# Mixture of experts behind a gated attention: experts 2 to 7 dealt out by their counts, the last three with 768 slots instead of 832

## The chip, the core and the metric

The kernel is one program on one core of a Trainium2 chip. The metric is the device time of one execution in microseconds (us), the median of the runs shown.

## The reference

A recurrent, gated attention (4 sequences, 8 heads, 768 steps, head size 40) gives 3072 rows `x` of 320 numbers. Each row is then sent to two of eight experts:

```
logits = x @ w_gate
noisy_logits = logits + np.log1p(np.exp(x @ w_noise)) * noise
top2 = np.argpartition(-noisy_logits, 2, axis=1)[:, :2]
top2_w = softmax of the two chosen noisy logits
for e in range(8):
    for k in range(2):
        mask = top2[:, k] == e
        h = np.maximum(x[mask] @ w1[e], 0.0)          # 320 -> 1024
        out[mask] += top2_w[mask, k, None] * (h @ w2[e])   # 1024 -> 320
```

There are 6144 choices, 768 for an expert on average. How many an expert gets (its count) is known only once the rows have been routed.

## The kernel before, in words

The attention runs in 24 units of 128 rows. While it runs, VectorE routes the rows (`g_part`): it finds the two best experts of each row and the row's rank within its expert, and a few one-hot matmuls turn expert and rank into a table TBL, 128 partitions by 8 x 7 columns: slot s of expert e stands in column 7e + s // 128, partition s % 128, and holds the row's number, or 0 where the slot is vacant. `decode` (L447) makes of columns of TBL the row numbers TOK, the choice masks KM and two helpers; vacant slots get a number beyond the last row.

An expert has a fixed number of slots, NT = 832 = 448 + 384, whatever its count: six tiles of 128 rows and one of 64 (`tiles`, L726; `rows_of`, L732). Its work:

- `gather` (L704): GpSimd's indirect DMAs fetch the rows of each tile (a vacant slot fetches nothing) into XG.
- `turn_x` and `spread_x` (L895, L902): VectorE transposes 32 x 32 blocks into XB, and 16 DMAs on SP's queue carry them to XT; `split_x` (L909) splits XT into a high part XH (ScalarE) and a low part XL (VectorE).
- `mm1` (L921): for each of the two halves of the slots (`parts`, L681) and each of eight blocks of 128 hidden units, eight matmuls (products of high and low parts) as wide as the half, 448 or 384 columns, at L931. ScalarE takes the high part HH of the result (L940), VectorE the low part HLO (L943). Of the 448 columns 64 go to HT instead (L950, L951), for the 64-row tile.
- `mm2` (L953): a tile of 128 rows is 24 matmuls of 320 columns (L960 to L962); the 64-row tile is 16, on HT (L968, L969), with ScalarE and VectorE adding its two halves (L970, L971). L973 applies the gate, `put` (L979) adds the 128 rows to the output by an indirect DMA.

Everything is written by hand into each engine's instruction stream, in the order of the text. While expert e is in `mm1` and `mm2`, the other engines prepare e + 1: its weights W1 go by SP's queue into RAW1 and are split at L149 and L150 (`split_w1`); W2 goes into RAW2 (`load_w2`, L686, issued after the first tile of e's `mm2`) and is split at L722 and L723 at the start of e + 1. The rows of e + 1 are gathered at the start of e, turned one tile after each `mm1` block from block 6 on (TURN), and split two steps at a time behind the third and later tiles of e's `mm2`. In `mm2` the tiles go in the order OR1 = 0, 6, 1, 2, 3, 4, 5.

Experts 0 and 1 are special: they begin while the routing still runs. Expert 0 is worked through in three parts (slots to 384, to 640, to 832) as the routing of rows advances; `advance` (L998) calls `decode` for a part when the table is done so far, the last call taking all columns from slot 640 of expert 0 to the end of expert 7. Expert 1 has halves of 512 and 320.

If an expert's count is over 832, a value `flag` (L614, read at L1129) sends the program through a slow loop over all experts (L1162) for the rows left over.

Of the kernel before, what the change touches and what calls it, by code (L numbers as in the profile page):

```python
# [7 lines left out]
F32 = mybir.dt.float32  # L8
# [50 lines left out]
def build(ctx, tc, qk, vk, fi, noise, wgn, w1, w2, cst, ce, out):  # L59
# [74 lines left out]

    def load_w1(e, ks=((0, 2), 2)):
        for k in ks:
            if k == 2:
                for p in range(2):
                    SP.dma_start(RAW1[64 * p:64 * p + 64, 2], w1[e, 256:320])
            else:  # L140
                a, b = k
                SP.dma_start(RAW1[:, a:b], w1[e, a * 128:b * 128].rearrange("(k p) f -> p k f", p=128))

    def split_w1(lo):
        for f in range(0, FF, 512):
# [45 lines left out]
    def run(steps):  # L191
        for _ in steps:
            pass
# [243 lines left out]
    def bc_part(t, b, late=False):  # L437
        if b:
# [5 lines left out]
                P.tensor_add(TBL, TBL, s)  # L444
            done[0] += len(b[0]) // 2

    def decode(a, b, more=True):  # L447

        t, n = TBL[:, a:b], slice(a, b)
        V.scalar_tensor_tensor(VC[:, n], t, 0.0, cs[:, C_VAC + a:C_VAC + b], op0=OP.is_equal, op1=OP.mult)  # L450
        V.scalar_tensor_tensor(AB[:, n], t, -1.0, t, op0=OP.mult, op1=OP.max)
        V.tensor_scalar(KM[:, n, 0], t, 0.0, None, op0=OP.is_gt)
        x = AB[:, n]
        if more:
            far = rt.tile([128, b - a], F32, name=f"far{a}", bufs=1)
            V.tensor_scalar(far, x, 0.5, FIT // 2, op0=OP.mult, op1=OP.add)
            x = rt.tile([128, b - a], F32, name=f"near{a}", bufs=1)
            V.scalar_tensor_tensor(x, AB[:, n], 0.0, far, op0=OP.add, op1=OP.min)
        V.scalar_tensor_tensor(TOK[:, n], x, -1.0, VC[:, n], op0=OP.add, op1=OP.add)
        V.tensor_scalar(KM[:, n, 1], t, 0.0, None, op0=OP.is_lt)  # L460

    def lc_part(i, t, w):
        u = i - 2
# [21 lines left out]
    def g_part(g):  # L485
# [121 lines left out]
        if u0 + nb == NU:  # L607
            V.tensor_add(rk[:, 0:1], rk[:, 0:1], bump[0])
            yield
            V.scalar_tensor_tensor(rk[:, 0:8], cs[:, C_I8:C_I8 + 8], -4096.0, rk[:, 0:8], op0=OP.mult, op1=OP.add)  # L610
            yield
            V.tensor_reduce(dd[:, 0:1], rk[:, 0:8], AX.X, OP.max)
            yield
            V.tensor_copy(flag, dd[:, 0:1])  # L614
# [64 lines left out]
        return psum.tile([128, 512], F32, name=name, bufs=2 if name in ("s0", "s1") else 1)  # L679

    def parts(e):  # L681
        s = (E0S, (0, 512, NT))[e] if e < 2 else (0, CA, NT)
        return [slice(a, b) for a, b in zip(s, s[1:])]


    def load_w2(e):  # L686
        SP.dma_start(RAW2, w2[e].rearrange("(j p) c -> p j c", p=128))

    def token(e, t):
        return TOK[0:rows_of(t), TC * e + t:TC * e + t + 1]  # L690
# [211 lines left out]
    def spread_x():  # L902
# [6 lines left out]
    def split_x():  # L909
        for h in range(2):  # L910
            c = slice(QO[2 * h], QO[2 * h] + 2 * QC[2 * h])
            fx = lambda a: a[:, c].rearrange("p (q t c) -> p q t c", q=2, c=32)
            fh = lambda a: a[:, c].rearrange("p (t q c) -> p q t c", q=2, c=32)
            for k in range(3):
                n = slice(0 if k < 2 else 64, 128)
                A.activation(fh(XH[n, k]), fx(XT[n, k]), AF.Copy)
                o = XL[:, k] if k < 2 else XH[0:64, 2]
                V.tensor_sub(fh(o), fx(XT[n, k]), fh(XH[n, k]).bitcast(F32))
                yield
# [137 lines left out]
    for f in range(8):  # L1057
        mm1(0, 1, f)
        advance(0.5, 2)
    assert done[0] == NU  # L1060
    load_w2(1)
    gather(1, ts=tiles(0, 1))
    for t in held:
# [22 lines left out]
    for e in range(1, NE):  # L1086
# [4 lines left out]
        for h in range(2):  # L1091
            for f in range(8):
# [22 lines left out]
        xs = split_x()  # L1115
        for n, t in enumerate(OR1):
            put(e, t, mm2(e, t))
            if e + 1 < NE:
                if not n:
# [40 lines left out]
                             in_=y[0:n], in_offset=None, compute_op=OP.add)  # L1160

    with tc.If(most > NT):  # L1162
        V.memset(ec, 0.0)
        with tc.For_i(0, NE, 1) as e:
            weights(e)
            x = xf[0:CS, 0:RW]
            tok = m2.tile([128, 1], I32, name="ftk")
            km = m2.tile([128, 2], F32, name="fkm")
            SP.dma_start(tok[0:CS], TOK[CS:128].rearrange("p (e c) -> p e c", e=NE)[:, bass.ds(e, 1), TC - 1:TC].rearrange("p e c -> p (e c)"))
            SP.dma_start(km[0:CS], KM[CS:128].rearrange("p (e c) k -> p e c k", e=NE)[:, bass.ds(e, 1), TC - 1].rearrange("p e k -> p (e k)"))  # L1170
            P.indirect_dma_start(out=x, out_offset=None, in_=XD, in_offset=bass.IndirectOffsetOnAxis(ap=tok[0:CS], axis=0),
                                 bounds_check=NTOK - 1, oob_is_err=False)
            V.tensor_mul(km[0:CS], km[0:CS], x[:, DM:DM + 2])
            V.tensor_add(km[0:CS, 0:1], km[0:CS, 0:1], km[0:CS, 1:2])
            plain(x, CS, km[0:CS, 0:1], tok[0:CS])
            V.tensor_scalar(ec, ec, 1.0, None, op0=OP.add)

        with tc.If(most > BLK):
            V.memset(ec, 0.0)
# [98 lines left out]
```

## Time and profile before

| | us |
|---|---|
| median of 3 runs | 543.9 (542.6 to 544.37) |
| span of the profiled execution, first to last instruction | 545.7 |
| TensorE busy in it | 521.9 |
| VectorE busy | 361.6 |
| ScalarE busy | 255.1 |
| GpSimd busy | 227.9 |

The profiled execution has no time of its own beside its span; the span is 1.8 us over the median of the runs. In the profile PE is TensorE's matmuls, PEld its weight loads, DVE VectorE, ACT ScalarE, POOL GpSimd and SP the engine that issues most DMAs; L931 is line 931 of the kernel. A row of a timeline gives start, duration, engine, line, operation and shapes, and in brackets how long the engine had been idle before it and what ended the wait. A matmul's duration overlaps that of the next; what it costs is the distance from one start to the next.

### The profile page before, as it was taken

To read this page: it belongs to the slowest core of one execution; us is meant where nothing else is said; L and a number is where in the kernel's file an instruction comes from. 1 tells how busy PE (TensorE), PEld (TensorE's weight loads), DVE (VectorE), ACT (ScalarE), POOL (GpSimd) and SP (SyncE) were. 2 spreads that over 40 slices of the span, in tenths; PEclk is the share of its full clock that TensorE was granted. 3 is DMA by queue.
4 is the path that set the end of the run, shared out by engine and by line. 5 is a ranking of instruction groups with operands and counts; after the bars stand their busy time and mean duration, and the time that the engine had idled before them with its cause. 6 is when DMAs were issued, how large, how long until landed. Compare 5 with 4: busy or idle time off the path is not lost.

```text
span 545.7 us, 13298 instructions
## 1 busy us (share of the span) xinstructions
PE 521.9 (96%) x5100; PEld 486.9 (89%) x5101; DVE 361.6 (66%) x983; ACT 255.1 (47%) x634; POOL 227.9 (42%) x282
## 2 busy tenths in 40 slices
PE   8889998988999899999999999999999999999995
PEld 3778887877989798999999999999999999999994
DVE  8988999998786377764854675485467548546411
ACT  8858877877614154432541543254154325415300
POOL 7445463164112837056224705632570563251043
PEclk9979999998999999999999999999999999999998
DMA  5898787897767626088159418614941771461033
GB/s 147 216 229 221 205 227 189 199 223 197 264 191 236 106 41 194 10 170 225 39 97 261 93 35 231 136 47 81 270 97 31 194 171 49 92 144 21 1 36 47
DMA packets 49797, 77.25 MB, mean 142 GB/s; under 512 B 10281, under 2 KB 39664, under 8 KB 49728
## 3 DMA queue, kind: packets, MB, share of 16 engines
q1 hardware_dynamic: 38464, 57.39, 37.9%
q0 software_dynamic: 11264, 18.95, 19.0%
q8 instruction: 42, 0.69, 0.5%
q14 instruction: 27, 0.22, 0.1%
HBM read 52.49 MB, written 17.73 MB: 129 GB/s over the span
## 4 chain that ended last, share of the span: by engine, by line
PE 73%; DVE 20%; issue 2%; DMA 1%; ACT 1%; POOL 1%; POOLq 0%; DVEq 0%; SPq 0%; ACTq 0%
PE s L931 24%; PE e L931 12%; PE o L960 5%; PE o L961 5%; PE o L962 5%; PE st L961 5%; PE st L960 4%; PE st L962 4%; DVE p L348 3%; DVE ob L602 2%; DVE kd L342 2%; DVE tm L382 1%; PE o L371 1%; PE st L969 1%; PE st L968 1%
## 5 line engine op out<-in xcount | busy, mean ns | idle before, releaser
L983 POOL DMA_INDIRECT y_out<-y,tok x56 | 92.3, 1647 | 194.8 <-DVE y L973 191.2
L940 ACT ACTIVATE hh<-s 128x384 fp32r<-128x384 f32 (+3 forms) x91 | 42.7, 470 | 83.0 <-PE s L931 80.7
L931 PE MATMUL s<-xh,w1h 128*128 128x384 f32 (+5 forms) x273 | 78.6, 345 | 0.9 <-DVE xh L743 0.8
L709 POOL DMA_INDIRECT xg<-rows,tok x56 | 63.0, 1125 | 29.2 <-issue 15.1
L931 PE MATMUL s<-xh,w1l 128*128 128x384 f32 (+5 forms) x273 | 64.3, 343 | 0.6 <-DVE xh L743 0.6
L943 DVE SCALAR_TENSOR_TENSOR hlo<-s,hh 128x384 fp32r<-128x384 f32 (+3 forms) x91 | 47.5, 522 | 20.1 <-ACT hh L940 16.6
L961 PE MATMUL o<-w2l,hh 128*128 128x320 f32 x192 | 59.8, 311 | 0.0
L960 PE MATMUL o<-w2h,hh 128*128 128x320 f32 x192 | 59.7, 311 | 0.0
L962 PE MATMUL o<-w2h,hlo 128*128 128x320 f32 x192 | 59.1, 308 | 0.0
L931 PEld LDWEIGHTS s<-xh,w1h 128*128 128x128 f32 x273 | 49.2, 188 | 4.0 <-ACT hh L940 1.0
L961 PE MATMUL st<-w2l,hh 128*128 128x320 f32 x168 | 52.3, 311 | 0.3 <-issue 0.3
L960 PE MATMUL st<-w2h,hh 128*128 128x320 f32 x168 | 52.1, 310 | 0.0
L962 PE MATMUL st<-w2h,hlo 128*128 128x320 f32 x168 | 51.7, 308 | 0.0
L931 PEld LDWEIGHTS s<-xh,w1l 128*128 128x128 f32 x273 | 48.4, 188 | 3.2 <-DVE xh L743 0.9
L931 PE MATMUL s<-xl,w1h 128*128 128x384 f32 (+5 forms) x182 | 47.6, 343 | 0.0
L383 POOL TENSOR_TENSOR xr<-tm,vk 128x320 f32<-128x320 f32 x24 | 21.3, 887 | 52.9 <-DVE tm L382 10.6
L973 DVE TENSOR_SCALAR y<-o,gw 128x320 f32<-128x320 f32 x24 | 13.2, 550 | 42.3 <-PE o L962 42.3
L931 PE MATMUL e<-xh,w1h 128*128 128x384 f32 (+5 forms) x135 | 39.6, 348 | 0.4 <-DVE ht L951 0.3
L973 DVE TENSOR_SCALAR y<-st,gw 128x320 f32<-128x320 f32 x21 | 11.6, 551 | 41.2 <-PE st L962 41.1
L940 ACT ACTIVATE hh<-e 128x384 fp32r<-128x384 f32 (+3 forms) x45 | 21.3, 473 | 34.6 <-PE e L931 24.9
L960 PEld LDWEIGHTS o<-w2h,hh 128*128 128x128 f32 x192 | 36.1, 188 | 0.3 <-DVE y L973 0.2
L962 PEld LDWEIGHTS o<-w2h,hlo 128*128 128x128 f32 x192 | 36.2, 188 | 0.0
(222 smaller groups left out, 1303.3 us busy)
## 6 DMA issues: line engine op xcount, KB each, us to landing
vk<-vk_in SPq DMA_DIRECT2D x48, 242.0 KB
raw<-w_in SPq DMA_DIRECT2D x7, 1280.0 KB
qk<-qk_in SPq DMA_DIRECT2D x48, 160.0 KB
raw<-w_in SPq DMA_DIRECT2D x7, 1024.0 KB
raw<-w_in SPq DMA_DIRECT2D x19, 256.0 KB
y_out<-zrow SPq DMA_DIRECT2D x15, 320.0 KB
xt__2782<-xb SPq DMA_DIRECT2D x24, 84.0 KB
rows<-xr POOLq DMA_DIRECT2D x12, 160.0 KB
```

The source lines that it names most:

```text
L342: V.tensor_mul(KD[u], VKS[u % 4][:, :, 328:648].rearrange("p x (h d) -> p x h d", h=H), W[u][:, :, :, L - 1:L].to_broadcast([128, 2, H, D]))
L348: V.tensor_mul(PP[u], SQ[u], W[u])
L383: P.tensor_mul(XR[u], tm.rearrange("p h d -> p (h d)"), SG[u % 4])
L709: P.indirect_dma_start(out=XG[0:rows_of(t), t], out_offset=None, in_=XD[0:n], in_offset=bass.IndirectOffsetOnAxis(ap=token(e, t), axis=0), ...
L931: T.matmul(ps[:, 0:n], l, r, start=i == 0, stop=i == len(ops) - 1)
L940: A.activation(hi, x, AF.Relu)
L943: V.scalar_tensor_tensor(lo, x, 0.0, hi.bitcast(F32), op0=OP.max, op1=OP.subtract)
L960: T.matmul(ps, HH[:, j, c], W2H[:, j], start=j == 0, stop=False)
L961: T.matmul(ps, HH[:, j, c], W2L[:, j], start=False, stop=False)
L962: T.matmul(ps, HLO[:, j, c], W2H[:, j], start=False, stop=j == 7)
L973: V.tensor_scalar(y[0:n], ps[0:n], GW[e][0:n, t:t + 1], None, op0=OP.mult)
L983: st = P.indirect_dma_start(out=out, out_offset=bass.IndirectOffsetOnAxis(ap=token(e, t), axis=0), in_=y[0:n], in_offset=None, compute_op= ...
```

## The change

On chip, as soon as the counts are known, VectorE ranks experts 2 to 7 by count (`POS`; ties go by number). `WHO` holds the expert at each rank, `SEL` is the permutation as a 6 x 6 one-hot. The places 2 to 7 of the program, which were experts 2 to 7, now stand for the experts by falling count: `deal` permutes the columns of TBL into TBP, and these are decoded. Weights are addressed by a register that SP loads from WHO. Places 2, 3 and 4 (`is_long`) keep 832 slots in 448 + 384; places 5, 6 and 7 have 768 slots in 384 + 384, six tiles, no 64-row tile. `flag` is taken from the counts with 64 added for the three short places, so that the slow loop is entered when a count is over 832 or that of a short place over 768. (That loop also changes: it takes up to 128 rows of each expert. It is left out of the diff.)

The decoding of places 2 to 7 moves: it was in the last `decode`, during the second part of expert 0, and now stands one step after each block of expert 0's third part.

```diff
     def load_w1(e, ks=((0, 2), 2)):
         for k in ks:
+            w = w1[weights_of(e)]
             if k == 2:
                 for p in range(2):
-                    SP.dma_start(RAW1[64 * p:64 * p + 64, 2], w1[e, 256:320])
+                    SP.dma_start(RAW1[64 * p:64 * p + 64, 2], w[:, 256:320].rearrange("e p f -> p (e f)"))
...
+    def deal():
+        x = rt.tile([128, NR, TC, NR], F32, name="dealt", bufs=1)
+        rows_ = TBL[:, EF * TC:].rearrange("p (e t) -> p t e", e=NR)
+        V.tensor_mul(x, SEL[:, :, None, :].to_broadcast([128, NR, TC, NR]), rows_[:, None].to_broadcast([128, NR, TC, NR]))
+        yield
+        V.tensor_reduce(TBP.rearrange("p (r t) -> p r t", r=NR), x, AX.X, OP.add)
+        yield
+        yield from decode_steps(EF * TC, NE * TC, True, TBP)
...
+            key = sm("key", [128, NR])
+            V.scalar_tensor_tensor(key, held, 8.0, i8[:, EF:8], op0=OP.mult, op1=OP.subtract)
+            yield
...
+            V.tensor_tensor(over, key[:, None, :].to_broadcast(sq), key[:, :, None].to_broadcast(sq), op=OP.is_gt)
+            yield
+            V.tensor_reduce(POS, over, AX.X, OP.add)
+            yield
+            V.tensor_tensor(SEL, POS[:, None, :].to_broadcast(sq), i8[:, 0:NR, None].to_broadcast(sq), op=OP.is_equal)
+            yield
+            V.tensor_mul(over, SEL, i8[:, None, EF:8].to_broadcast(sq))
+            yield
+            with nc.allow_low_precision(reason="whole numbers under 8"):
+                V.tensor_reduce(WHO, over, AX.X, OP.add)
+            yield
+            V.tensor_scalar(key, POS, LONG - 0.5, float(CS), op0=OP.is_gt, op1=OP.mult)
+            yield
+            V.tensor_add(held, held, key)
...
-        s = (E0S, (0, 512, NT))[e] if e < 2 else (0, CA, NT)
+        s = (E0S, (0, 512, NT))[e] if e < EF else (0, CA, NT) if is_long(e) else (0, NM // 2, NM)
...
+    def weights_of(e):
+        if e < EF:
+            return slice(e, e + 1)
+        if e not in whose:
+            whose[e] = nc.values_load(WHO[0:1, e - EF:e - EF + 1], engines=[mybir.EngineType.SP], min_val=EF, max_val=NE - 1,
+                                      skip_runtime_bounds_check_because="a sum of one-hot products with EF to NE - 1")
+        return bass.ds(whose[e], 1)
+
+    def is_long(e):
+        return e < EF + LONG
...
-            return range(7)
+            return range(7 if is_long(e) else 6)
...
-    QC = (224, 224, 192, 192)
-    QO = (0, 224, 448, 640)
+    def quarters(e):
+        return ((224, 224, 192, 192), (0, 224, 448, 640)) if is_long(e) else ((192,) * 4, (0, 192, 384, 576))
...
-                decode(E0S[h] // 128, E0S[h + 1] // 128 if h < 2 else NE * TC)
+                decode(E0S[h] // 128, E0S[h + 1] // 128 if h < 2 else EF * TC)
...
     for f in range(8):
         mm1(0, 2, f)
+        next(dealing, None)
...
-                if TURN <= 8 * h + f < TURN + 7 and e + 1 < NE:
+                if e + 1 < NE and 8 * h + f - TURN in tiles(e + 1):
                     turn_x(8 * h + f - TURN)
-                    if 8 * h + f == TURN + 6:
-                        spread_x()
+                    if 8 * h + f - TURN == tiles(e + 1)[-1]:
+                        spread_x(e + 1)
                         weigh(e + 1)
...
-        for n, t in enumerate(OR1):
+        for n, t in enumerate(x for x in OR1 if x in tiles(e)):
             put(e, t, mm2(e, t))
```

Three places where the instructions move. First VectorE in the third part of expert 0, its first blocks (`hlo` and `ht` evacuate a block; `xl`, `xh` belong to a transposed tile of expert 1; `dealt` and `tbp` are the product and its sum over experts). Before:

```order
L943 SCALAR_TENSOR_TENSOR hlo<-e,hh 128x128
L951 SCALAR_TENSOR_TENSOR ht<-e,ht 128x64
L742 TENSOR_TENSOR xl<-s_3442,xh 128x2x128
L743 TENSOR_TENSOR xh<-s_3442,xh 64x128
L943 SCALAR_TENSOR_TENSOR hlo<-s_3449,hh 128x128
L951 SCALAR_TENSOR_TENSOR ht<-s_3449,ht 128x64
L943 SCALAR_TENSOR_TENSOR hlo<-s_3462,hh 128x128
L951 SCALAR_TENSOR_TENSOR ht<-s_3462,ht 128x64
```

And after, the same blocks:

```order
L1011 SCALAR_TENSOR_TENSOR hlo<-e,hh 128x128
L1019 SCALAR_TENSOR_TENSOR ht<-e,ht 128x64
L487 TENSOR_TENSOR dealt<-sel,tbl 128x252
L808 TENSOR_TENSOR xl<-s_3458,xh 128x2x128
L809 TENSOR_TENSOR xh<-s_3458,xh 64x128
L1011 SCALAR_TENSOR_TENSOR hlo<-s_3465,hh 128x128
L1019 SCALAR_TENSOR_TENSOR ht<-s_3465,ht 128x64
L489 TENSOR_REDUCE tbp<-dealt 128x42
L1011 SCALAR_TENSOR_TENSOR hlo<-s_3479,hh 128x128
L1019 SCALAR_TENSOR_TENSOR ht<-s_3479,ht 128x64
L456 SCALAR_TENSOR_TENSOR vc<-tbp,cs 128x42
```

One more instruction stands behind the evacuation of every block, and the next block's evacuation waits its turn behind it.

Second, SP's queue between two experts: the last of the transposed rows (`xt`), then W2 (`raw` from L687) and the next W1 (`raw` from L142 and L139). Before:

```order
L907 DMA xt__2782<-xb 32x2x192 x2
L907 DMA xt__2782<-xb 32x3x192 x2
L687 DMA raw_2777<-w_in 128x8x320
L142 DMA raw_116<-w_in 128x2x1024
L139 DMA raw_116<-w_in 64x1024 x2
```

And after (ISA rows are register instructions of SP):

```order
L974 DMA xt__2786<-xb 32x2x192 x2
L974 DMA xt__2786<-xb 32x3x192 x2
L753 ISA
L753 DMA raw_2781<-w_in 128x8x320
L745 TENSOR_LOAD who
L150 ISA
L150 DMA raw_120<-w_in 128x2x1024
L147 ISA
L147 DMA raw_120<-w_in 64x1024
```

The register load stands behind W2 and ahead of the next W1.

Third, VectorE in the last tiles of `mm2` of expert 6, with the split of expert 7's rows (`xl`, `xh` from `xt`). Before:

```order
L973 TENSOR_SCALAR y<-o,gw 128x320
L918 TENSOR_TENSOR xh<-xt__2782,xh 64x2x7x32
L918 TENSOR_TENSOR xl<-xt__2782,xh 128x2x6x32
L973 TENSOR_SCALAR y<-st,gw 128x320
L918 TENSOR_TENSOR xl<-xt__2782,xh 128x2x6x32
L918 TENSOR_TENSOR xh<-xt__2782,xh 64x2x6x32
L973 TENSOR_SCALAR y<-o,gw 128x320
L973 TENSOR_SCALAR y<-st,gw 128x320
L943 SCALAR_TENSOR_TENSOR hlo<-s_6566,hh 128x6x64
```

And after:

```order
L1041 TENSOR_SCALAR y<-st,gw 128x320
L986 TENSOR_TENSOR xh<-xt__2786,xh 64x2x6x32
L986 TENSOR_TENSOR xl<-xt__2786,xh 128x2x6x32
L1041 TENSOR_SCALAR y<-o,gw 128x320
L986 TENSOR_TENSOR xl<-xt__2786,xh 128x2x6x32
L986 TENSOR_TENSOR xh<-xt__2786,xh 64x2x6x32
L1041 TENSOR_SCALAR y<-st,gw 128x320
L1011 SCALAR_TENSOR_TENSOR hlo<-s_6517,hh 128x6x64
```

Behind the last split stood two more tiles before the next expert's first block; now one does.

More of the change, by code (lines that the diff above doesn't have):

```diff
@@ L37 @@
 NB = 4
+EF, LONG = 2, 3
+NR = NE - EF
 STEP, SHARE = 0.19, 1.65
@@ L90, in build @@
     flag = keep.tile([128, 1], I32, name="flag")
+    POS = keep.tile([128, NR], F32, name="pos")
+    WHO = keep.tile([128, NR], I32, name="who")
+    SEL = keep.tile([128, NR, NR], F32, name="sel")
+    TBP = keep.tile([128, NR * TC], F32, name="tbp")
     early = ctx.enter_context(tc.tile_pool(name="early", bufs=1))
@@ L445, in bc_part, with decoding @@
             done[0] += len(b[0]) // 2
-    def decode(a, b, more=True):
[L449 to L460, printed above, removed]
+    def decoding(t, vac, tok, km, vc, ab, more, pool, name):
+        V.scalar_tensor_tensor(vc, t, 0.0, vac, op0=OP.is_equal, op1=OP.mult)
+        yield
+        V.scalar_tensor_tensor(ab, t, -1.0, t, op0=OP.mult, op1=OP.max)
+        yield
+        V.tensor_scalar(km[:, :, 0], t, 0.0, None, op0=OP.is_gt)
+        yield
+        x = ab
+        if more:
+            shape = [128, ab.shape[1]]
+            far = pool.tile(shape, F32, name=f"far{name}", bufs=1)
+            V.tensor_scalar(far, x, 0.5, FIT // 2, op0=OP.mult, op1=OP.add)
+            yield
+            x = pool.tile(shape, F32, name=f"near{name}", bufs=1)
+            V.scalar_tensor_tensor(x, ab, 0.0, far, op0=OP.add, op1=OP.min)
+            yield
+        V.scalar_tensor_tensor(tok, x, -1.0, vc, op0=OP.add, op1=OP.add)
+        yield
+        V.tensor_scalar(km[:, :, 1], t, 0.0, None, op0=OP.is_lt)
+        yield
@@ new lines, in decode_steps @@
+    def decode_steps(a, b, more=True, t=None):
+        n = slice(a, b)
+        t = TBL[:, n] if t is None else t
+        return decoding(t, cs[:, C_VAC + a:C_VAC + b], TOK[:, n], KM[:, n], VC[:, n], AB[:, n], more, rt, a)
+    def decode(a, b, more=True):
+        run(decode_steps(a, b, more))
+    def deal():
[6 more added lines that the diff above has]
+        yield from decode_steps(EF * TC, NE * TC, True, TBP)
@@ L1060, in build @@
     assert done[0] == NU
+    while routing:
+        fill(1.0)
+    dealing = deal()
     load_w2(1)
@@ L1114, in build @@
             P.tensor_mul(OVM[:, :, 2:4], WTS[:, :, 0:2], ov)
-        xs = split_x()
-        for n, t in enumerate(OR1):
+        xs = split_x(e + 1) if e + 1 < NE else iter(())
+        for n, t in enumerate(x for x in OR1 if x in tiles(e)):
             put(e, t, mm2(e, t))
@@ L1162, in build @@
     with tc.If(most > NT):
-        V.memset(ec, 0.0)
+        left = m2.tile([128, NE], F32, name="left")
+        V.memset(left, 1.0)
+        V.memset(left[0:NM + 128 - NT, 0:EF], 0.0)
+        V.tensor_scalar(left[0:NM + 128 - NT, EF:], POS[0:NM + 128 - NT], LONG - 0.5, None, op0=OP.is_gt)
+        V.tensor_mul(left, left, TBL.rearrange("p (e c) -> p e c", e=NE)[:, :, TC - 1])
+        ltok = m2.tile([128, NE], I32, name="ltok")
+        lkm = m2.tile([128, NE, 2], F32, name="lkm")
+        lvc, lab = (m2.tile([128, NE], F32, name=n) for n in ("lvc", "lab"))
+        vac = cs[:, C_VAC:C_VAC + NE * TC].rearrange("p (e c) -> p e c", e=NE)[:, :, TC - 1]
+        run(decoding(left, vac, ltok, lkm, lvc, lab, True, m2, "l"))
         with tc.For_i(0, NE, 1) as e:
             weights(e)
-            x = xf[0:CS, 0:RW]
+            x = xf[:, 0:RW]
             tok = m2.tile([128, 1], I32, name="ftk")
             km = m2.tile([128, 2], F32, name="fkm")
-            SP.dma_start(tok[0:CS], TOK[CS:128].rearrange("p (e c) -> p e c", e=NE)[:, bass.ds(e, 1), TC - 1:TC].rearrange("p e c -> p (e c)"))
-            SP.dma_start(km[0:CS], KM[CS:128].rearrange("p (e c) k -> p e c k", e=NE)[:, bass.ds(e, 1), TC - 1].rearrange("p e k -> p (e k)"))
-            P.indirect_dma_start(out=x, out_offset=None, in_=XD, in_offset=bass.IndirectOffsetOnAxis(ap=tok[0:CS], axis=0),
+            SP.dma_start(tok, ltok[:, bass.ds(e, 1)])
+            SP.dma_start(km, lkm[:, bass.ds(e, 1)].rearrange("p e k -> p (e k)"))
+            P.indirect_dma_start(out=x, out_offset=None, in_=XD, in_offset=bass.IndirectOffsetOnAxis(ap=tok, axis=0),
                                  bounds_check=NTOK - 1, oob_is_err=False)
[L1173 to L1176, printed above, removed]
+            V.tensor_mul(km, km, x[:, DM:DM + 2])
+            V.tensor_add(km[:, 0:1], km[:, 0:1], km[:, 1:2])
+            plain(x, 128, km[:, 0:1], tok)
         with tc.If(most > BLK):
```

24 lines of the change are left out of this document (20 added, 4 removed).

## The prediction

> **What bounds the kernel now.** I read the page first, then the windows by stage, then the chain of waits in order of time, then timelines where stages meet. The page and the windows (us, then the busy time of PE, PEld, DVE, ACT and POOL with their instructions, the granted clock, the DMA engines' share and GB/s):
>
> ```profile
> PE 521.9 (96%) x5100; PEld 486.9 (89%) x5101; DVE 361.6 (66%) x983; ACT 255.1 (47%) x634; POOL 227.9 (42%) x282
> 395.00:442.90 47.90, 47.90 (x290) 46.77 (x289) 28.38 (x68) 18.44 (x45) 20.58 (x21) 1.00 0.53 128
> 442.90:490.80 47.90, 47.90 (x290) 46.77 (x289) 28.46 (x68) 18.44 (x45) 20.76 (x21) 1.00 0.45 94
> ```
>
> A window here is one expert, 47.90 us from block 0 to block 0 of the next, and PE is busy in all of it, at full clock; the others have 19 us and more to spare. So from expert 1 on, time is the distance between matmul starts, and nothing else. The chain gives that distance for one block of mm1 (eight matmuls), 448 columns in the first half and 384 in the second:
>
> ```profile
> 446.38 1.64 PE e L931 x8
> 460.47 1.41 PE e L931 x8
> ```
>
> The timeline of the last expert gives the 64-row tile (first of its 16 matmuls to the first of the next tile) and the tiles of 128 rows (from one gate, which waits for the tile's last matmul, to the next):
>
> ```profile
> 518.82 0.31 PE L968 MATMUL st<-w2h,ht 128*128 128x320 f32 x1
> 521.17 0.31 PE L960 MATMUL o<-w2h,hh 128*128 128x320 f32 x1
> 531.93 0.55 DVE L973 TENSOR_SCALAR y<-o,gw 128x320 f32<-128x320 f32 x1 [2.97 <-PE o L962]
> 535.45 0.55 DVE L973 TENSOR_SCALAR y<-st,gw 128x320 f32<-128x320 f32 x1 [2.97 <-PE st L962]
> ```
>
> That is 2.35 us for the small tile and 3.52 for a full one. An expert should then take 8 x 1.64 + 8 x 1.41 + 6 x 3.52 + 2.35 = 47.87 us; the window says 47.90. The sum closes, so it can be cut term by term.
>
> **The three short places.** They lose the small tile, 2.35 us, and in eight blocks 64 of 448 columns, 8 x (1.64 - 1.41) = 1.84 us: 4.19 us a place, 12.6 us for three. All of it lies on the path.
>
> The Trainium skill (TensorE: Matmul & The Clock Gate, section Back-to-back issue gap) puts the isolated gap at N / 2.4 + 2.5 ns for N columns. By it, as an estimate, a place saves 64 x 26.7 ns + 16 x 135.8 ns = 3.9 us, three save 11.6, and the forecast would be 532.7. The rows are longer than the rule (1.41 us / 8 = 176 ns against 162.5), so I keep the rows.
>
> ScalarE and VectorE lose the small instructions on HT and its tile, GpSimd three gathers and three additions; these engines wait already, so I count nothing.
>
> **Ranking the counts, in expert 0's second part.** Eight small instructions more on DVE. Rows of the groups by shape, for these and the decoding, and of the timeline where they go:
>
> ```profile
> L610 DVE SCALAR_TENSOR_TENSOR rk<-cs,rk 128x8 f32<-128x8 f32 x1 | 0.2, 169 | 0.0
> L582 DVE TENSOR_REDUCE rank<-oh 128x8 int32<-128x64 f32 x6 | 1.3, 219 | 0.1
> L450 DVE SCALAR_TENSOR_TENSOR vc<-tbl,cs 128x51 f32<-128x51 f32 x1 | 0.2, 212 | 0.0
> L742 DVE TENSOR_TENSOR xl<-st,xh 128x256 fp32r<-128x256 f32 x1 | 0.4, 424 | 0.0
> 169.03 0.42 DVE L943 SCALAR_TENSOR_TENSOR hlo<-s,hh 128x256 fp32r<-128x256 f32 x1 [0.85 <-ACT hh L940]
> 170.94 0.42 DVE L943 SCALAR_TENSOR_TENSOR hlo<-e,hh 128x256 fp32r<-128x256 f32 x1 [0.47 <-ACT hh L940]
> ```
>
> At 0.17 to 0.22 us each they are some 1.6 us, spread over five blocks between evacuations that wait for ACT (0.85 and 0.47 us idle before the two shown); PE has no wait in these blocks. Cost zero; without that cover, 1.6. In return the decoding that frees the gathers has 9 columns instead of 51: seven instructions, each up to 0.05 us shorter (212 against 163 for two to three columns). Gathers start some 0.2 us sooner, and PE has one wait in this stretch that may be for them, without a named releaser:
>
> ```profile
> PE s L739 <- issue: 0.4, 1, 0.4
> PE e L931 <- DVE ht L951: 0.3, 1, 0.3
> PE s L931 <- DVE xh L743: 1.4, 2, 0.8
> ```
>
> Gain 0 to 0.4, taken as 0.2.
>
> **Dealing, in expert 0's third part.** Here PE already waits for DVE (the two rows above), since a block of 192 columns takes PE only some 1.1 us (two from 191.09 to 193.57 below, with a transpose and a wait between). The timeline:
>
> ```profile
> 191.09 0.44 PE L931 MATMUL e<-xh,w1h 128*128 128x192 f32 x2 [0.33 <-DVE ht L951]
> 193.57 0.44 PE L931 MATMUL s<-xh,w1h 128*128 128x192 f32 x2 [0.16 <-DVE ht L951]
> 191.10 0.42 DVE L742 TENSOR_TENSOR xl<-s,xh 128x256 fp32r<-128x256 f32 x1 [0.15 <-ACT xh L741]
> 192.45 0.23 DVE L951 SCALAR_TENSOR_TENSOR ht<-s,ht 128x64 fp32r<-128x64 f32 x1 [0.29 <-ACT ht L950]
> 193.20 0.23 DVE L951 SCALAR_TENSOR_TENSOR ht<-s,ht 128x64 fp32r<-128x64 f32 x1 [0.29 <-ACT ht L950]
> ```
>
> `dealt` (252 products) and `tbp` (a sum of 252) are each priced at 0.42 us, by the row of 256 elements; the nearest reduction, of 64, is 0.22. They stand ahead of the evacuation of blocks 1 and 2. Block 5 of PE, at 193.57, waits for block 2's `ht` (193.20 + 0.23). That one comes 0.84 us later less the 0.15 that `xl` waits for ACT anyway: 0.7. PE had 0.16 of waiting there, which is the same wait and moves with it; I take 0.6. Behind it each block carries one decoding step of 0.2 us on top of the 0.75 from one `ht` to the next: 0.95 us of DVE against 1.1 of PE, so no more is lost. Bounds: 0, if the spare banks take it up, and 1.2, if every step ahead of block 5 and one behind it counts in full.
>
> **SP's register loads.** Six times SP reads an expert's number, ahead of W1. The only register load in the trace stands at the end, and SP's waits show the longest time around it:
>
> ```profile
> SPq L1162 <- SPq L1162: 5.4, 2, 4.9
> 429.11 0.53 SPq L687 DMA_DIRECT2D raw<-w_in x1
> 429.74 0.62 SPq L142 DMA_DIRECT2D raw<-w_in x1
> 462.37 0.62 ACT L149 ACTIVATE w1h<-raw 128x512 fp32r<-128x512 f32 x1
> ```
>
> So a load costs between nothing and 4.9 us on SP. Queued behind it is W1, then only the transposed rows of half an expert later. W1 of expert 7 is issued at 429.74 and first read at 462.37, 32 us later, for a transfer that ends by about 444 (below): cost zero, and 4.9 late would still leave 13 us.
>
> **The short boundaries.** Preparation is tied to tiles, so with fewer tiles it comes nearer the end. In the row split, DVE's last piece follows the fifth tile of mm2:
>
> ```profile
> 436.09 0.55 DVE L973 TENSOR_SCALAR y<-o,gw 128x320 f32<-128x320 f32 x1 [1.72 <-PE o L962]
> 437.14 0.55 DVE L918 TENSOR_TENSOR xh<-xt__2782,xh 64x384 fp32r<-64x384 f32 x1
> ```
>
> It ends 1.6 us after its tile. Two tiles followed (7.04 us, slack 5.4); now one does (3.52, slack 1.9). Not late: zero.
>
> W2 and the next W1 leave SP at 429.11 and 429.74. The windows show how long the DMA engines are busy with both, and the timeline ACT's first evacuation and first read of W2 in expert 7:
>
> ```profile
> 440.00:442.00 2.00, 2.00 (x16) 2.00 (x15) 0.16 (x1) 0.00 (x0) 1.56 (x2) 1.00 1.01 243
> 442.00:444.00 2.00, 2.00 (x14) 1.92 (x13) 0.55 (x1) 0.00 (x0) 0.15 (x2) 1.00 0.83 102
> 444.00:446.00 2.00, 2.00 (x11) 1.83 (x10) 0.56 (x1) 0.55 (x2) 1.70 (x2) 1.00 0.01 1
> 444.83 0.49 ACT L940 ACTIVATE hh<-s 128x384 fp32r<-128x384 f32 x1 [12.15 <-PE s L931]
> 446.19 0.47 ACT L722 ACTIVATE w2h<-raw 128x320 fp32r<-128x320 f32 x1
> ```
>
> Both have landed by about 443.7, 14.6 us after the first issue; W2 is read 2.5 us later. In a short place the issue is one block earlier (1.41 us) against mm2's start, and mm2 is 2.35 shorter; the next read, without the HT step between (446.19 against 444.83 + 0.49) and with a block 0.23 shorter, comes some 1.1 sooner. If W2 landed last of the two, 2.5 + 1.41 - 2.35 - 1.1 leaves 0.5 us; as it is issued first, more. Zero.
>
> **Sum.** 12.6 - 0.6 + 0.2 = 12.2 us. The profiled execution should have a span of 545.7 - 12.2 = 533.5; the median of the runs lies 1.8 below the span of that execution, so 543.9 - 12.2 = 531.7. The tail does not change: the last matmul starts at 538.63 and the span ends 7.1 later, in both.
>
> ```profile
> 538.63 0.31 PE L962 MATMUL o<-w2h,hlo 128*128 128x320 f32 x1
> ```
>
> **Rivals.**
>
> *The short boundaries wait.* If W2 lands last, and the pair takes a seventh longer than 14.6 us (2.1 us, less 0.5 of slack), ACT stands at its first read, with block 1's evacuation behind it, and PE runs out of banks. Two boundaries follow a short place (5 to 6 and 6 to 7); at 1.6 us each, 534.9. For it: the DMA engines are at 1.0 to the end of that stretch. Against it: order of issue, and no wait of ACT for W2 anywhere now. 0.10.
>
> *Weight loads are the limit.* PEld is busy 46.77 of 47.90 us. If that sets the pace, narrower blocks with as many loads gain nothing and only the small tiles fall away: 3 x 2.35 - 0.4 = 6.7, 537.2. Against it: blocks with the same eight loads take 1.64 and 1.41 us. 0.03. This is what the Trainium skill (Perfetto Trace Analysis, section Identifying the Most-Contended Engine) would suggest, which judges TensorE by the share of LDWEIGHTS and not of matmuls.
>
> *The slow loop runs: slower.* It decides at one number: if the third smallest count of experts 2 to 7 is over 768 (or any over 832), the flag sends the program through the loop over eight experts. Each loads its own weights first, with nothing before it to hide them; the pair took 14.6 us above, so 8 x 14.6 = 117 us at least: 649 or more. The counts can be read from the bytes of the software queue while an expert's rows are gathered (experts 3, 5 and 7, each with one 128-row addition of 0.164 MB):
>
> ```profile
> q0 software_dynamic: 464, 1.16, 24.6%
> q0 software_dynamic: 464, 1.20, 34.0%
> q0 software_dynamic: 464, 1.18, 31.6%
> ```
>
> At 336 numbers of 4 bytes a row: 741, 771 and 756, each within 4. The reference's rule on its drawn inputs gives 722, 742, 815, 769, 783, 752 for experts 2 to 7. The third smallest is 752, 16 below the bound. That is also the case in which the change would not do what it says (a wrong order puts 815 rows in a short place). 0.03.
>
> *A wait that eats all of it*, unseen in this trace: 0.01, no change.
>
> **Numbers.** The forecast has 0.83. Its own range takes the bounds, 11.4 to 13.0 us, and the scatter of the runs, 0.9 either way: 530.0 to 533.4. To hold the first rival as well the range goes to 535.0; what lies outside has 0.07. Under 0.3% (1.6 us) is what a measurement can't tell from no change. Faster 0.96, same 0.01, slower 0.03.
>
> **What would show it.** Windows of 43.7 us for places 5 and 6, with PE busy throughout, and 47.9 for 2 to 4; no L968 rows in the last three; PE's wait for `ht` in expert 0's third part grown by about 0.6; no wait of ACT for W2, none of PE at the boundaries. I am wrong if the short windows are over 44.5, if that third part loses over 1.2, or if the stretch ahead of it moves by over a microsecond.

## The result, and the profile after

The changed kernel takes 532.56 us (median of 4 runs, 530.18 to 534.58) against 544.13 us for the kernel before (4 runs, 542.60 to 548.88). The ratio is 0.9745, with a 95% interval of 0.9696 to 0.9793: between 11 and 17 us off. The profiled execution took 530.18 us, 528.4 of it span. The forecast of 531.7 was 0.9 us under the median.

The page of the changed kernel, its line of busy times:

```profile
PE 504.4 (95%) x5053; PEld 473.5 (90%) x5053; DVE 353.3 (67%) x964; ACT 249.6 (47%) x607; POOL 218.7 (41%) x273
```

PE falls by 17.5 us of busy time, the span by 17.3: what went was matmul time and not waiting. (Of the 17.5 us, 2.9 lie ahead of expert 0's mm1, where the code is the same and the granted clock was 0.99 in this profile and 0.96 in the one before: PE was busy 121.81 us there, for 124.68.) Where it went is read from windows that begin and end at matmul starts (busy time of PE, PEld, DVE, ACT, POOL, then the clock, the DMA share and GB/s). Before, the first runs from the first matmul of expert 0's mm1 to that of expert 1, and the second is one of the six later experts:

```profile
138.62:202.96 64.34, 61.26 (x433) 56.05 (x430) 43.00 (x181) 24.13 (x74) 23.40 (x27) 1.00 0.60 166
...
251.25:299.17 47.92, 47.92 (x290) 46.79 (x289) 28.36 (x68) 18.44 (x45) 20.59 (x21) 1.00 0.56 135
```

The changed kernel, the same stretch, then places 3 and 4 (long), 5 and 6 (short):

```profile
134.94:199.95 65.01, 60.65 (x433) 55.86 (x430) 45.09 (x198) 24.18 (x74) 23.37 (x27) 1.00 0.60 169
...
295.85:343.57 47.72, 47.72 (x290) 46.77 (x289) 28.27 (x68) 18.27 (x45) 20.84 (x21) 1.00 0.52 128
343.57:391.29 47.72, 47.72 (x290) 46.78 (x289) 27.61 (x66) 18.11 (x45) 19.43 (x20) 1.00 0.52 125
391.29:434.78 43.49, 43.49 (x275) 43.49 (x273) 25.12 (x56) 16.89 (x36) 17.32 (x18) 1.00 0.53 136
434.78:478.26 43.48, 43.48 (x274) 43.48 (x273) 25.18 (x56) 16.89 (x36) 17.23 (x18) 1.00 0.44 99
```

A short place is 4.23 us shorter than a long one of the same execution, with 15 or 16 fewer matmul records (the small tile's) and PE busy in all of it. Finding the order shows in the first row, 65.01 for 64.34. And the long places, which the change leaves as they were, are 0.20 us shorter than before: that was in no step of the prediction. The chain gives it block by block, the first two rows being the halves of a long place and the third a block of a short one:

```profile
345.35 1.62 PE e L999 x8
...
359.50 1.41 PE e L999 x8
...
395.65 1.40 PE e L999 x8
```

A block of 448 columns takes 1.62 us where it took 1.64. Those of 384 differ by a hundredth from place to place, which eight of them together show better. Here are the second halves of places 2, 4 and 5:

```profile
261.19:272.37 11.18, 11.18 (x66) 11.18 (x64) 10.37 (x31) 6.28 (x15) 0.28 (x2) 1.00 0.04 9
356.52:367.82 11.30, 11.30 (x66) 11.30 (x64) 10.28 (x29) 6.27 (x15) 0.00 (x0) 1.00 0.06 16
402.47:413.65 11.18, 11.18 (x65) 11.18 (x65) 9.92 (x27) 5.85 (x12) 0.00 (x0) 1.00 0.10 28
```

The kernel before has 11.30 us here (360.23 to 371.53 in its trace). In the short places, and in the second half of place 2 (a long one), eight blocks of 384 columns are 0.12 us shorter.

The two profiles differ by 17.26 us of span, and the windows share it out: 3.68 us ahead of expert 0's mm1 (138.62 against 134.94), -0.67 from there to expert 1, 0 in expert 1, 0.71 in places 2 to 4, and 13.54 from place 5 to the end. The first term is not the change's: the code up to there is the same, and over all twelve profiles of this study that start lies anywhere between 134.9 and 145.1. What is left, 13.6 us, is the change.

### The profile page after: what moved, and what is told of

Same layout as the page of the kernel before. It is cut to its first block, busy times and chain, and to the rows that moved or that the text cites. A ratio compares the mean times of both kernels' runs of the same rounds, so it can differ in the third digit from the quotient of the medians.

```text
span 528.4 us, 13181 instructions
## 1 busy us (share of the span) xinstructions
PE 504.4 (95%) x5053; PEld 473.5 (90%) x5053; DVE 353.3 (67%) x964; ACT 249.6 (47%) x607; POOL 218.7 (41%) x273
## 4 chain that ended last, share of the span: by engine, by line
PE 73%; DVE 17%; ACT 3%; DMA 3%; issue 2%; SPq 1%; POOL 0%; POOLq 0%; DVEq 0%; ACTq 0%
PE s L999 24%; PE e L999 11%; PE o L1028 5%; PE o L1029 5%; PE o L1030 5%; PE st L1029 5%; PE st L1028 5%; PE st L1030 5%; DVE p L356 3%; DVE ob L633 3%; DVE kd L350 2%; PE o L379 1%; DMA vk<-vk_in 1%; DVE tm L390 1%; PE s L342 1%
## 5 line engine op out<-in xcount | busy, mean ns | idle before, releaser
L1051 POOL DMA_INDIRECT y_out<-y,tok x53 | 87.1, 1643 | 191.7 <-DVE y L1041 188.7
L999 PE MATMUL s<-xh,w1h 128*128 128x384 f32 (+5 forms) x273 | 76.8, 338 | 1.4 <-DVE vc L456 0.7
L775 POOL DMA_INDIRECT xg<-rows,tok x53 | 59.4, 1121 | 28.1 <-issue 13.7
L999 PE MATMUL s<-xh,w1l 128*128 128x384 f32 (+5 forms) x273 | 62.5, 336 | 0.7 <-DVE xh L809 0.7
L1029 PE MATMUL o<-w2l,hh 128*128 128x320 f32 x184 | 57.3, 311 | 0.0
L1028 PE MATMUL o<-w2h,hh 128*128 128x320 f32 x184 | 57.2, 311 | 0.0
L1030 PE MATMUL o<-w2h,hlo 128*128 128x320 f32 x184 | 56.6, 308 | 0.0
L1029 PE MATMUL st<-w2l,hh 128*128 128x320 f32 x176 | 54.9, 312 | 0.7 <-issue 0.7
L1028 PE MATMUL st<-w2h,hh 128*128 128x320 f32 x176 | 54.5, 310 | 0.2 <-issue 0.2
L1030 PE MATMUL st<-w2h,hlo 128*128 128x320 f32 x176 | 54.1, 307 | 0.2 <-issue 0.2
L999 PEld LDWEIGHTS s<-xh,w1h 128*128 128x128 f32 x273 | 48.9, 188 | 3.5 <-ACT hh L1008 0.9
L999 PEld LDWEIGHTS s<-xh,w1l 128*128 128x128 f32 x273 | 47.9, 188 | 2.3 <-DVE xh L809 0.9
L999 PE MATMUL s<-xl,w1h 128*128 128x384 f32 (+5 forms) x182 | 46.4, 336 | 0.0
L999 PE MATMUL e<-xh,w1h 128*128 128x384 f32 (+5 forms) x135 | 38.7, 340 | 0.3 <-DVE ht L1019 0.3
L1028 PEld LDWEIGHTS o<-w2h,hh 128*128 128x128 f32 x184 | 34.6, 188 | 0.3 <-DVE y L1041 0.2
```

Source lines behind the costliest of these rows:

```text
L775: P.indirect_dma_start(out=XG[0:rows_of(t), t], out_offset=None, in_=XD[0:n], in_offset=bass.IndirectOffsetOnAxis(ap=token(e, t), axis=0), ...
L999: T.matmul(ps[:, 0:n], l, r, start=i == 0, stop=i == len(ops) - 1)
L1028: T.matmul(ps, HH[:, j, c], W2H[:, j], start=j == 0, stop=False)
L1029: T.matmul(ps, HH[:, j, c], W2L[:, j], start=False, stop=False)
L1030: T.matmul(ps, HLO[:, j, c], W2H[:, j], start=False, stop=j == 7)
L1051: st = P.indirect_dma_start(out=out, out_offset=bass.IndirectOffsetOnAxis(ap=token(e, t), axis=0), in_=y[0:n], in_offset=None, compute_op= ...
```

## The experiments

The theory under test was the prediction's: a short place saves its narrow blocks (1.84 us) and its small tile (2.35 us) in full, finding the order costs about half a microsecond in one wait of PE, and nothing else moves. The rivals were the weight loads as the limit, the short boundaries waiting, and the slow loop. A later one was that the unforeseen 0.2 us a place come from the new order. A ratio is to the kernel before, run beside the variant on the same chip, with its 95% interval.

**The kernel before, once more**, as a measure of how two profiles of one program differ.

> The kernel before, unchanged, for a second profile. The sum says: windows of 47.9 us for experts 2 to 7 and PE's waits in expert 0's third part as before. The rival, that the pace of an execution wanders by itself, says that an expert's window comes out between 47.6 and 47.9, and the first matmul of expert 1, at 202.96 in the first profile, up to 4 us elsewhere.

Measured: 546.67 us, 0.9979 (0.9944 to 1.0014). Its windows:

```profile
137.99:202.34 64.35, 61.16 (x433) 56.05 (x431) 42.71 (x181) 24.20 (x74) 23.38 (x27) 1.00 0.61 170
...
442.31:490.23 47.92, 47.92 (x291) 46.80 (x289) 28.48 (x68) 18.44 (x45) 20.75 (x21) 1.00 0.45 94
```

From expert 0 on they repeat to 0.01 us. So 0.67 and 0.20 us between windows are differences, though single times of this program lie anywhere from 543.65 to 551.50 us (19 runs).

**The order fixed by hand**, with no ranking and no dealing:

```diff
+ORDER = (0, 1, 4, 6, 5, 7, 3, 2)
-    (ranking block, WHO loads, deal())
+    (token lists, sums and weights of ORDER[e]; decode to NE * TC; dealing = iter(()))
```

> Leaves out finding the order on chip: the order 4, 6, 5, 7, 3, 2 is written into the program, nothing is ranked, dealt or loaded into registers, and all columns are decoded where they were before. The sum says 12.6 us under the kernel before, the 64-row tiles and narrow blocks alone, and about 0.6 under the changed kernel, with PE's wait in expert 0's third part back at that of before (0.16 ahead of block 5). If finding the order cost more than its visible wait (register loads ahead of W1, for one), this gains 2 us or more on the changed kernel.

Measured: 533.61 us, 0.9726 (0.9672 to 0.9779). Its windows, expert 0's stretch and a short place, and the start of block 5 in expert 0's third part:

```profile
145.13:209.48 64.35, 61.09 (x433) 55.81 (x432) 43.02 (x181) 24.26 (x74) 23.41 (x27) 1.00 0.60 166
...
400.82:444.31 43.49, 43.49 (x274) 43.49 (x273) 25.11 (x56) 16.89 (x36) 17.33 (x18) 1.00 0.54 135
```

```profile
200.08 0.44 PE L980 MATMUL s<-xh,w1h 128*128 128x192 f32 x2 [0.17 <-DVE ht L1000]
```

Without the search for the order the stretch is back at 64.35, block 5's wait at 0.17 (0.16 before), and the short place is the same. The time can't be told from that of the changed kernel. (Its profile starts expert 0 late, at 145.13; that is the stretch ahead, which scatters.)

**The order alone**, with all six places long:

```diff
-EF, LONG = 2, 3
+EF, LONG = 2, 6
```

> The order is found and dealt, but all places keep 832 slots. The sum says 0.4 to 0.7 us slower than the kernel before, within the scatter of the runs, with all windows at 47.7 to 47.9. If register loads or the deal stall PE elsewhere, windows longer than 47.9 or a time over 546.

Measured: 546.42 us, 0.9976 (0.9937 to 1.0014).

```profile
139.61:204.27 64.66, 60.86 (x433) 55.93 (x432) 45.51 (x201) 24.10 (x74) 23.42 (x27) 1.00 0.60 166
...
395.61:443.33 47.72, 47.72 (x290) 46.77 (x289) 28.28 (x68) 18.30 (x45) 20.88 (x21) 1.00 0.51 127
```

The order alone can't be told from no change by its times. Its cost is in the first row. Over the six profiles that rank and deal at these places, the third chip's left out (65.01 for the changed kernel, 64.66 here, and 65.85, 64.60, 65.04 and 64.47 for the next variants), the stretch has a mean of 64.94 us, against 64.35 for the three without the search: 0.59, though single profiles lie 0.1 to 1.5 above. What repeats in all six is one step: from block 4 to block 5 of expert 0's third part pass 1.83 to 1.86 us, and 1.27 to 1.29 in the three without. The long places are at 47.72 here too, so their 0.2 us have nothing to do with the short ones.

**Narrow blocks alone**, the small tile kept in every place:

```diff
-        return range(7 if is_long(e) else 6)
+        return range(7)
```

> The short places keep a 64-row tile of vacant slots (its work is done on stale data, and its rows fall beyond the output), but their first halves have 384 columns. The sum says 46.0 us for the window of a short place against 47.8 for a long one, and 3 x 1.84 - 0.6 = 4.9 us under the kernel before, near 539. Weight loads as the limit say equal windows, and no gain: 544.

Measured: 539.87 us (4 runs), 0.9829 (0.9770 to 0.9888). A long and a short place:

```profile
348.56:396.28 47.72, 47.72 (x291) 46.77 (x289) 28.08 (x68) 18.11 (x45) 20.68 (x21) 1.00 0.52 125
396.28:442.12 45.84, 45.84 (x291) 45.84 (x289) 26.43 (x60) 17.22 (x37) 19.95 (x21) 1.00 0.53 131
```

The same 289 records of weight loads, and 1.88 us less. PEld is busy in all of the short place here and is still not the limit. This run's page gives a load in mm1 (L999) and one in mm2 (L1028) the same length, 188 ns:

```profile
L999 PEld LDWEIGHTS s<-xh,w1h 128*128 128x128 f32 x273 | 48.9, 188 | 3.6 <-ACT hh L1008 1.0
L1028 PEld LDWEIGHTS o<-w2h,hh 128*128 128x128 f32 x192 | 36.1, 188 | 0.3 <-DVE y L1041 0.2
```

Yet the matmuls of a full tile of mm2, each with a load of its own, start 147 ns apart (24 in 3.52 us), and those of the short blocks 175 ns apart (8 in 1.40 us). So loads overlap each other, and their row can be full without setting the pace. That decides against the weight loads as the limit. The Trainium skill (Perfetto Trace Analysis, section Identifying the Most-Contended Engine) would have suggested them, as it judges TensorE by the share of peak flops and the busy share of LDWEIGHTS, and not by that of matmuls. This trace does not agree: that share went up, from 46.77 of 47.72 us to 45.84 of 45.84, while the window fell by 1.88.

The small tile makes the rest, 45.84 - 43.49 = 2.35 us. By windows against the kernel before, this variant should save 3 x (47.92 - 45.84) + 0.71 for places 2 to 4 - 0.59 = 6.4 us; the interval of its times is 6.1 to 12.6, so they can't confirm it closely.

**The changed kernel, once more.**

> The changed kernel again, for a second profile and a narrower interval. The sum says 12.0 us under the kernel before, a ratio of 0.978; short windows 4.2 us under the long ones of the same execution. If the larger difference of the two first profiles (17.3 us) is the change's own, the ratio is 0.968.

Measured: 532.35 us (6 runs), 0.9740 (0.9699 to 0.9781). The 0.978 of the sum lies just inside this interval and the 0.968 just outside. Expert 0's mm1 starts at 136.10 and takes 64.60 us to expert 1.

**The row split one tile later** in the short places, so that the slack of the boundary is used up:

```diff
-            if n > 1:
+            if n > (1 if is_long(e) else 2):
```

> Behind the short places the rows of the next are split one tile later, so that the last two pieces follow the last tile. By the step on the boundaries (slack 1.9 us) these pieces end about 1.6 us after the last tile and PE waits up to 1.6 us at two boundaries: 3 us slower than the changed kernel, and windows of 45 us. The rival: the last pieces belong to the second half of the columns, which PE reads only 11 us into the next place, so the slack was never 1.9 us, and the time does not change.

Measured: 534.25 us (4 runs), 0.9757 (0.9704 to 0.9810). Place 6 in the windows, whose rows are split behind the short place 5, and the last piece of that split in the timeline:

```profile
439.21:482.69 43.48, 43.48 (x274) 43.48 (x273) 25.18 (x56) 16.91 (x36) 17.44 (x18) 1.00 0.45 99
```

```profile
440.45 0.55 DVE L986 TENSOR_TENSOR xh<-xt__2786,xh 64x384 fp32r<-64x384 f32 x1
```

Nothing moved, although the last piece now ends at 441.00, 1.8 us after place 6 has begun (439.21). The rival was right: this piece belongs to the second half of the columns, and PE comes to that half only after eight blocks, 11.18 us into the place. So the slack was never 1.9 us.

**The row split two tiles later**, with the pieces left over after the last tile (one run, on a third chip):

```diff
-            if n > (1 if is_long(e) else 2):
+            if n > (1 if is_long(e) else 3):
+        for _ in xs: pass
```

> Behind the short places the rows of the next are split two tiles later than in the changed kernel; the two pieces left over follow the last tile. The last piece of the first half now ends 1.1 to 1.7 us after the last tile. If PE's first block is what needs the first half, PE waits 1 to 2 us at the boundaries 5 to 6 and 6 to 7, with windows of 44.5 to 45.5 us. If the split has still more room, 43.5 stays.

Measured: 527.77 us, beside 542.58 for the kernel before on that chip. Place 6 in the windows, and the boundary ahead of it in the timeline:

```profile
431.01:475.14 44.13, 43.60 (x274) 43.28 (x273) 25.18 (x56) 16.89 (x36) 17.09 (x18) 1.00 0.45 98
```

```profile
431.80 0.55 DVE L986 TENSOR_TENSOR xh<-xt__2786,xh 64x384 fp32r<-64x384 f32 x1
...
432.40 0.44 PE L999 MATMUL s<-xh,w1h 128*128 128x384 f32 x1 [0.53 <-DVE xh L986]
```

Now PE waits for the split rows, 0.53 us, and the place is 0.65 longer (44.13 for 43.48). This time the piece is the last of the *first* half. It is read by the fifth matmul of the place's first block, and not by the first: that matmul starts 1.39 us after the place (431.01), where it started 0.70 after it in the changed kernel. The boundary has room for one more tile of delay and not for two.

**Four short places**, with the fourth smallest count too large for one, so that the program's own flag sends it through the loop:

```diff
-EF, LONG = 2, 3
+EF, LONG = 2, 2
```

> Four short places instead of three. The fourth count from the end is 769, one row over 768, so the flag is set and the slow loop runs. The fast part should be 4.2 us shorter still, near 527, and the loop cost at least 8 x 14.6 = 117 us on top: 645 or more. If the loop is cheap (below 17 us), the rival that was priced as slower than before would not have been.

Measured: 857.44 us (one run). The window from about the fast part's end:

```profile
525.00:855.00 330.00, 177.72 (x536) 126.22 (x536) 32.58 (x112) 0.00 (x0) 21.03 (x16) 0.58 0.21 60
```

Eight experts in 330 us are 41 us each, with PE busy in 54% of it at a granted clock of 0.58. So this rival, had it come true, would have been slower by far, as it was priced; its 649 "or more" was only a floor, 208 us below the measured time. In the changed kernel the loop does not run.

**Dealing ahead of expert 0**, so that `dealt`, `tbp` and the decoding stand behind the counting and not beside the blocks of the third part:

```diff
-    dealing = deal()
+    dealing = iter(())
...
     for t in held: put(0, t, held[t])
+    run(deal())
```

> The deal and its decoding in one piece ahead of mm2 of expert 0's second part, where DVE has idle stretches of 1.8 and 3.4 us. The sum says that PE's wait of 0.74 us ahead of block 5 falls back to 0.16 and nothing else moves: 0.6 us under the changed kernel. If transposed tiles are then late, PE waits at the start of the third part instead, and the time is the same or worse.

Measured: 531.42 us (6 runs, one of them 538.25; 529.89 for the other five), 0.9712 (0.9669 to 0.9756) by those five. Its stretch of expert 0, and block 5 in the timeline:

```profile
136.53:199.49 62.96, 60.49 (x433) 55.70 (x432) 46.05 (x201) 24.13 (x73) 23.70 (x27) 1.00 0.61 171
```

```profile
190.11 0.44 PE L999 MATMUL s<-xh,w1h 128*128 128x192 f32 x2 [0.17 <-DVE ht L1019]
```

Block 5's wait is back at 0.17, so the dealing, with the decoding behind it, was its cause. The stretch gives back more than that: 62.96 is 1.4 us under the kernel before, and all of that lies ahead of block 5 (190.11 - 136.53 = 53.58 us, against 193.57 - 138.62 = 54.95 before). Why is open: it lies between the second part's start and block 1 of the third, which takes 21.0 us here and 22.3 before, but anything from 21.9 to 23.3 in the six profiles named above. As one profile of it stands here and its interval overlaps that of the changed kernel (0.9699 to 0.9781), this version is at least as good as the change, and not shown to be better.

**The kernel before with the same four small tiles**, set to zero once and never read, 360 bytes a partition:

```diff
+    POS, WHO, SEL, TBP = (the four tiles of the change)
+    for x in (POS, WHO, SEL, TBP): P.memset(x, 0)
```

> The kernel before, with the four small tiles of the change (360 bytes of a partition) set aside in the same place, set once and not used. Everything that is set aside behind them, W1's two parts among it, moves up by them as in the changed kernel. If the place of the operands sets the pace, blocks of 448 columns fall from 1.64 to 1.62 us and an expert's window from 47.9 to 47.7, some 1.5 us in all. If something else in the changed kernels does, 1.64 and 47.9 stay.

Measured: 541.26 us, 0.9973 (0.9941 to 1.0005), on the third chip. Its stretch of expert 0, one of its experts, the second half of another (eight blocks of 384 columns), and a block of 448 columns in its chain:

```profile
136.97:197.09 60.12, 59.22 (x434) 55.50 (x432) 43.68 (x181) 24.42 (x74) 23.72 (x27) 1.00 0.64 178
...
293.10:340.81 47.71, 47.71 (x290) 46.76 (x289) 28.27 (x68) 18.29 (x45) 20.86 (x21) 1.00 0.53 129
401.48:412.78 11.30, 11.30 (x65) 11.29 (x64) 10.36 (x31) 6.28 (x15) 0.28 (x2) 1.00 0.03 9
```

```profile
250.39 1.62 PE e L937 x8
```

Nothing of the change but its memory (and the four instructions that clear it) is in this kernel, and it has the faster pace of the long places: 47.71 for 47.92, 1.62 for 1.64. So these 0.2 us come from where the operands lie, and the rival, the new order, falls. No profile of the kernel before was taken on this chip; but the long places of the changed kernel are at 47.72 on all three, so the chip is not the reason. The faster blocks of 384 columns are not in this kernel: eight take 11.30 us, as before, and 11.18 in the short places. Their cause stays open.

## Why the prediction was right, point by point

**What bounds the kernel.** Right. In every variant without the loop, a place from 2 on is the sum of its matmul distances, but for the wait that the split two tiles later makes.

**The three short places, 4.19 us each.** Right in mechanism and size: 4.23 in one execution, of which 1.88 for the narrow blocks (priced 1.84) and 2.35 for the tile (priced 2.35). That the 1.88 comes so near its price is in part luck: the eight blocks that were narrowed give 1.77 of it (12.95 us for the first half of place 4, 11.18 for that of place 5), and the rest comes from the second half, whose columns the change leaves alone. The rows that were kept, and not the 3.9 us worked out from the Trainium skill's gap rule (TensorE: Matmul & The Clock Gate, section Back-to-back issue gap), gave the time.

**Ranking, cost 0 and gain 0.2.** From expert 0's first matmul to block 5 of its third part pass 55.64 us (190.58 - 134.94), 54.95 before. Block 5's wait, next, takes 0.58 of the 0.69; 0.11 is left. That is a balance, though, and not the ranking's own price. From the second part's start to the third's pass 0.78 us more (20.42 for 19.64): in its mm2 PE waits five times without a named releaser, 1.68 us in all, for two times and 0.69 before. The third part then gives back 0.62 between its first two blocks (2.07 for 2.69). Over the six profiles, the time from mm1's start to block 5, less 0.58 for its wait, lies between 0.45 us under the kernel before and 0.92 over it, with a mean of 0.0. So a cost of zero agrees with the runs, but half a microsecond more or less could hide in them. The first gather starts 6.20 us after the second part's first matmul, for 6.40 before: 0.2 sooner, as forecast, but no gain from it can be seen.

**Dealing, 0.6 in one wait.** Right in place and size, the size with some luck. The timeline of the changed kernel:

```profile
187.30 0.62 DVE L487 TENSOR_TENSOR dealt<-sel,tbl 128x252 f32<-128x252 f32 x1
189.31 0.40 DVE L489 TENSOR_REDUCE tbp<-dealt 128x42 f32<-128x252 f32 x1
190.21 0.22 DVE L1019 SCALAR_TENSOR_TENSOR ht<-s,ht 128x64 fp32r<-128x64 f32 x1 [0.29 <-ACT ht L1018]
190.58 0.44 PE L999 MATMUL s<-xh,w1h 128*128 128x192 f32 x2 [0.74 <-DVE vc L456]
```

PE waits 0.74 us for 0.16: 0.58 more. The view names `vc`, the first step of the decoding, which DVE did between `ht` (done at 190.43) and the matmul; what the matmul needs is `ht`, as the prediction had it. `dealt` was dearer than its price (0.62 for 0.42), `tbp` was not (0.40): together 1.02 us for 0.84, and PE's wait grew by the forecast 0.6 all the same. From block 5 to expert 1 both kernels take 9.4 us (199.95 - 190.58 and 202.96 - 193.57), so nothing more is lost behind it.

**SP's register loads, 0.** Right. W2 and W1 in SP's queue, with the load between them:

```profile
421.48 0.40 SPq L753 DMA_DIRECT2D raw<-w_in  x1
...
422.47 0.38 SPq L150 DMA_DIRECT2D raw<-w_in  x1
```

From 421.88 to 422.47 are 0.59 us, where 0.10 stood before: near the lower of the bounds (nothing to 4.9), and 0.5 us against a slack of over 13.

**The short boundaries, 0.** Right in cost, wrong in the slack of the row split. The timeline at the end of place 5: the last pieces of the split's two halves (428.52, 432.50), the matmuls of place 6 that read them first (435.48, 446.65), and ACT's first evacuation and first read of W2:

```profile
428.52 0.55 DVE L986 TENSOR_TENSOR xh<-xt__2786,xh 64x384 fp32r<-64x384 f32 x1
...
432.50 0.56 DVE L986 TENSOR_TENSOR xh<-xt__2786,xh 64x384 fp32r<-64x384 f32 x1
...
435.48 0.34 PE L999 MATMUL s<-xh,w1h 128*128 128x384 f32 x1
...
436.37 0.49 ACT L1008 ACTIVATE hh<-s 128x384 fp32r<-128x384 f32 x1 [11.53 <-PE s L999]
436.89 0.47 ACT L788 ACTIVATE w2h<-raw 128x320 fp32r<-128x320 f32 x1
...
446.65 0.34 PE L999 MATMUL e<-xh,w1h 128*128 128x384 f32 x1
```

The last piece ends at 433.06, 1.7 us ahead of place 6 (434.78), near the 1.9 that was worked out. But I took the start of the place for the moment at which that piece is needed. It belongs to the second half, which is first read by block 8: its reader starts at 446.65, 13.6 us later. The piece that counts is the last of the first half, which ends at 429.07 and is read at 435.48: a slack of 6.4 us. The two delays bear this out. One tile (3.52 us) changed nothing; two (7.04) are 0.6 more than the slack, and place 6 grew by 0.65.

W2 is read at 436.89, straight behind `hh`, without a wait, as forecast, and so it is in place 7 (480.38, where `hh` ends at 480.35). The prediction's rows at 444.83 and 446.19 are expert 6's and not, as it says, expert 7's; its working is the same for both.

**What the sum lacked.** The pace. Places 2 to 4 are 0.71 us shorter together: 0.2 each by the blocks of 448 columns, and 0.1 by the second half of place 2. A short place is 4.43 us under a place of the kernel before (47.92 - 43.49) and not 4.19, as its blocks of 384 columns are faster too. By windows the change is worth 3 x 4.43 + 0.71 - 0.59 = 13.4 us, against 12.2 in the sum; the difference is this term, less the 0.2 of the gathers. The sum took the pace of each width of block as fixed, and the profile of before, which has one pace for each in experts 2 to 7, gave no sign that it was not.

The median came 0.9 us *above* the forecast all the same, since the two medians of the result lie 11.6 us apart and not 13.4. Runs scatter by more than the 0.9 either way that I took from three of them: the 19 runs of one program spread over 7.9 us. So the mechanism was right, but that the time lies within a microsecond of the forecast is luck: a missing term and the scatter nearly cancelled.

**A test that was badly set.** I was to be wrong if the stretch ahead moved by over a microsecond. Up to expert 0's mm1 it moved by 3.68, with the same code, and over the twelve profiles its end lies anywhere in ten microseconds. Only the part from that matmul on (0.11 us to block 5, without its wait) could be a test.

## What to carry to other kernels

Where one engine is busy in all of a stretch, price a cut by its own rows of start-to-start distance, term by term, and check that the terms close on the window before one of them is taken out; here that gave 4.19 for 4.23. A piece of work is late by the moment at which its own reader starts, and not by the start of the stage. Small work that is put beside short blocks costs what its longest instruction delays the evacuation next behind it; the small work ahead of those blocks, the ranking, showed no cost. Compare stages by windows within one execution or between matmul starts, not by whole times, when the stretch ahead of the change scatters by more than the change's smaller terms.

## What the runs showed of the hardware

The pace of a matmul stream depends on where its operands lie: 360 bytes of unread tiles made eight matmuls of 448 columns go from 1.64 to 1.62 us, each time in all kernels that had them, on three chips, at a granted clock of 1.00 throughout. In the padded kernel the blocks of 384 columns stayed as they were (11.30 us for eight). Which operand it is, and why, stays open. So does the faster pace of 384 columns in the changed kernel, 11.18 us for eight in the short places and in place 2 (which is why that place takes 47.61 us), where the padded kernel's place 2 keeps 47.72.

Weight loads overlap: loads of 188 ns went with matmuls that start 147 ns apart, each with its own load.

On the third chip the stretch from expert 0's mm1 to expert 1 takes 60.12 us in the padded kernel and 60.71 in the changed one with the late split, 4 us less than in the profiles before them, while the later experts keep their 47.72. The difference of the two is 0.59 again, but one profile of each stands here, and block 5's wait is 0.18 and not 0.74. Five waits of PE that the kernel before has from the second part's mm2 to block 5 of the third part (0.16 to 0.78 us each, 2.0 in all) are gone in the padded kernel's profile; the rest of the 4 us was not traced, and whether the chip makes it or the time of the run is open.

The loop's stretch was granted a clock of 0.58, where the fast part had 1.00, although PE was busy in only 54% of it. Nothing was tried on that.
